# Retention and channel mix on one core: the order of instructions taken from a list schedule computed when the kernel is built

## The chip, the cores and the metric

The kernel runs on one core of a Trainium2 chip. A core has five engines with instruction streams of their own: PE (TensorE, matrix products into PSUM), DVE (VectorE), ACT (ScalarE), POOL (GpSimd) and SP (SyncE, which here only issues DMAs). Each engine takes its instructions in the order in which they were written into its stream, and waits at an instruction until what it needs has been signalled by the others. The metric is the device time of one execution, in microseconds (us); lower is better.

## What is computed

A retention layer (a linear attention with a decaying state) over q, k and v of shape 4 x 8 heads x 768 x 64, and then a channel mix (RWKV's feed-forward part) over its output, as 4 x 768 x 512:

```python
gamma = 1.0 - 2.0 ** (-5.0 - np.arange(H))
for t in range(S):
    state = gamma * state + einsum('bhd,bhe->bhde', k[:, :, t], v[:, :, t])
    y[:, :, t] = 1 / sqrt(D) * einsum('bhd,bhde->bhe', q[:, :, t], state)
x = y.transpose(0, 2, 1, 3).reshape(B, S, H * D)
x_prev = concatenate([0, x[:, :-1]], axis=1)
xk = mu_k * x + (1 - mu_k) * x_prev
xr = mu_r * x + (1 - mu_r) * x_prev
k = maximum(xk @ w_k, 0)            # 512 -> 1024
v = k * k @ w_v                     # 1024 -> 512
r = 1 / (1 + exp(-(xr @ w_r)))      # 512 -> 512
out = r * v
```

## The kernel before

A batch's 768 positions are cut into six chunks of 128 for the attention and into three blocks of 256 for the channel mix: 24 chunks and 12 blocks in all. Numbering below is over the whole run (chunk 0 to 23, block 0 to 11); block m needs chunks 2m and 2m + 1.

*A chunk* (`attention`, lines 105 to 167). Three DMAs bring q, k and v as 256 KB each into `t32` (line 100). DVE scales q and k by powers of gamma into float16, `qks` (line 108); POOL casts v (line 112). PE transposes `qks` in eight pieces into PSUM, `pT` (line 116), and ACT copies that out as `qkT` (line 118). PE forms the scores `pA` (line 123), DVE masks them in two halves into `a2t` (line 129). PE adds up the state `pS` from this chunk's k and v (line 136) and, through a product with the identity, the old state (line 142); DVE scales it into `s_new` (line 147). The output `pY` is the old state times q (line 155) plus scores times v (line 161); ACT copies it into `xT`, the transposed activations of the batch (line 166).

*A block* (`moe_block`, lines 169 to 223). POOL takes the difference of neighbouring positions, `dx` (line 174). DVE mixes it with mu into `x16` for k and for r, four instructions each (line 179). PE multiplies by w_k into four tiles `pZ`, 32 matmuls (line 192); ACT applies the ReLU into `krel` (line 196) and squares pairs of tiles into `k2` (line 201). For each half of the block's positions PE forms `pR` (four matmuls, line 206), ACT its sigmoid `rsb` (line 211), PE `pV` (eight matmuls, line 214), DVE the product of the two, `osb` (line 219), and SP issues the store (line 223).

*The order.* The program is written chunk after chunk, with a block behind every second chunk and the weights' loads and casts behind chunk 0. Tile's scheduler then sets each engine's order and the waits. PSUM is divided by pools: two banks shared by `pT`, `pS` and `pY`, two for `pA`, four for the block's tiles. On SP, the loads of chunk 1 stand behind the three weight loads (5.2 MB).

Of the kernel before, what the change touches and what calls it, by code (L numbers as in the profile page):

```python
# [9 lines left out]
F16 = mybir.dt.float16  # L10
# [4 lines left out]
KSC = 64.0  # L15


@with_exitstack
def kernel(
# [12 lines left out]
    nc = tc.nc  # L32
# [26 lines left out]
    wpool = ctx.enter_context(tc.tile_pool(name="weights", bufs=1))  # L59
    xpool = ctx.enter_context(tc.tile_pool(name="xstage", bufs=2))  # L60
# [3 lines left out]
    psX = ctx.enter_context(tc.tile_pool(name="psX", bufs=2, space=bass.MemoryType.PSUM))  # L64
    psA = ctx.enter_context(tc.tile_pool(name="psA", bufs=2, space=bass.MemoryType.PSUM))
    psM = ctx.enter_context(tc.tile_pool(name="psM", bufs=4, space=bass.MemoryType.PSUM))

# [4 lines left out]
    nc.sync.dma_start(out=c32, in_=c32d.ap())  # L72
    nc.sync.dma_start(out=c16, in_=c16d.ap())
# [5 lines left out]
    nc.sync.dma_start(out=mu[:, 0], in_=moe_mu_k.rearrange("(co ci) -> ci co", ci=P))  # L79
    nc.sync.dma_start(out=mu[:, 1], in_=moe_mu_r.rearrange("(co ci) -> ci co", ci=P))  # L80

    wk16 = wpool.tile([P, NCO, dff], F16, name="wk16")
    wv16 = wpool.tile([P, NFO, dm], F16, name="wv16")
    wr16 = wpool.tile([P, NCO, dm], F16, name="wr16")

    def load_weights():
        wk32 = wpool.tile([P, NCO, dff], F32, name="wk32")
        wr32 = wpool.tile([P, NCO, dm], F32, name="wr32")
        wv32 = wpool.tile([P, NFO, dm], F32, name="wv32")
        nc.sync.dma_start(out=wk32, in_=moe_w_k.rearrange("(co ci) f -> ci co f", ci=P))  # L90
        nc.sync.dma_start(out=wr32, in_=moe_w_r.rearrange("(co ci) e -> ci co e", ci=P))
        nc.sync.dma_start(out=wv32, in_=moe_w_v.rearrange("(fo fi) e -> fi fo e", fi=P))
        nc.vector.tensor_copy(out=wk16, in_=wk32)
        nc.scalar.copy(out=wr16, in_=wr32)
        nc.gpsimd.tensor_copy(out=wv16, in_=wv32)

    def load(b, c):
        t = ld.tile([P, 3, H, D], F32, tag="qkv32")
        for i, src in enumerate((q, k, v)):
            nc.sync.dma_start(  # L100
                out=t[:, i], in_=src[b, :, c * C : (c + 1) * C, :].rearrange("h t d -> t h d")
            )
        return t

    def attention(b, c, xT, s_prev):
        t32 = load(b, c)
        qks = awork.tile([P, 2, H, D], F16, tag="qks")
        nc.vector.tensor_tensor(  # L108
            out=qks, in0=t32[:, 0:2], in1=Gqk.unsqueeze(3).broadcast_to([P, 2, H, D]), op=ALU.mult
        )  # L110
        v16 = awork.tile([P, H, D], F16, tag="v16")
        nc.gpsimd.tensor_copy(out=v16, in_=t32[:, 2])  # L112
        pT = psX.tile([P, 2, NJ, C], F16, tag="px")
        for j in range(NJ):
            for i in range(2):
                nc.tensor.transpose(pT[:, i, j, :], qks[:, i, 2 * j : 2 * j + 2, :], ident)  # L116
        qkT = awork.tile([P, 2, NJ, C], F16, tag="qkT")
        nc.scalar.copy(out=qkT, in_=pT)  # L118
        pA = [psA.tile([P, NJ, C], F32, tag="pA", name=f"pA{hp}") for hp in range(2)]
        for j in range(NJ):  # L120
# [104 lines left out]
    for b in range(B):  # L225
# [3 lines left out]
        for c in range(NCH):  # L229
            s_prev = attention(b, c, xT, s_prev)  # L230
            if b == 0 and c == 0:
                load_weights()
# [32 lines left out]
```

## Time and profile before

| | |
|---|---|
| median of 2 runs | 259.45 us (259.04 to 259.86) |
| the profiled execution | 260.24 us |
| its span, first to last instruction | 257.6 us |
| busy: PE, DVE, ACT, POOL | 189.0, 126.7, 104.6, 42.3 us |
| mean granted clock of PE | 0.878 |
| moved by DMA | 30.73 MB, 119 GB/s over the span |

The span is what the profile shows; the rest of an execution's time lies around it. In the rows of the profile a group is named by its line, engine, operation and tiles (`pT<-c_sb,qks` is written from the constants and `qks`; buffer numbers and digits are left out, so `x16` reads `x`, `k2` reads `k`, `t32` reads `t`). Behind it stand the count, and in brackets the time for which the engine had waited just before, with what released it. PE is a matmul, PEld the load of its stationary operand, which overlaps. SPq is SP issuing a DMA. Rows of busy time by stretch give start and end, length, the engines' busy times with their instruction counts, the granted clock of PE (1.00 is full), the busy share of the DMA engines, and GB/s. Ends of matmuls are modelled.

### The profile page before, as it was taken

How to read it: one execution, taken by the hardware profiler on the slowest of the kernel's cores; microseconds unless marked ns; L12 is line 12 of the kernel's file. 1: busy time of each engine (PE TensorE's matmuls, PEld its weight loads, DVE VectorE, ACT ScalarE, POOL GpSimd, SP SyncE). 2: the span in 40 equal slices, each digit the busy share in tenths (PEclk: the TensorE clock that was granted, in tenths of full speed). 3: DMA queues.
4: the chain of work that ended last, by engine and by line, in shares of the span. 5: the costliest groups of instructions: out<-in, count | busy, mean ns of one | idle time of the engine just before them, and what ended most of it. 6: DMA issues, size and time to landing. Idle time of an engine off the chain costs nothing. (4 is left out here: it accounts for less than half of the span.)

```text
span 257.6 us, 3978 instructions
## 1 busy us (share of the span) xinstructions
PE 189.0 (73%) x1632; PEld 118.4 (46%) x1632; DVE 126.7 (49%) x217; ACT 104.6 (41%) x147; POOL 42.3 (16%) x41
## 2 busy tenths in 40 slices
PE   0300677779859969869679899789699599797394
PEld 0200445446336446455455564555464464563251
DVE  0431547357366375574680681771672762542422
ACT  1130221924534535337317326435345445344070
POOL 0105340030040040040130230310310400200200
PEclk9999999997986997999958959959869959779598
DMA  5999995149396374655366266265341101101002
GB/s 101 371 371 279 219 213 130 41 137 192 90 213 150 80 168 88 158 119 104 108 122 125 81 122 125 94 116 129 101 95 43 41 3 41 41 3 67 15 0 81
DMA packets 81793, 30.73 MB, mean 119 GB/s; under 512 B 76528, under 2 KB 76656, under 8 KB 81776
## 3 DMA queue, kind: packets, MB, share of 16 engines
q1 hardware_dynamic: 81776, 30.50, 49.7%
q8 instruction: 12, 0.20, 0.3%
q14 instruction: 5, 0.04, 0.0%
HBM read 24.20 MB, written 6.29 MB: 118 GB/s over the span
## 5 line engine op out<-in xcount | busy, mean ns | idle before, releaser
L192 PE MATMUL pZ<-x,wk 128*128 128x256 f16 x384 | 66.3, 354 | 13.8 <-DVE x L179 13.8
L192 PEld LDWEIGHTS <-wk 128*128 128x128 f16 x384 | 48.3, 126 | 30.8 <-issue 14.3
L219 DVE SCALAR_TENSOR_TENSOR osb<-pV,rsb 128x512 f32<-128x512 f32 x24 | 16.6, 691 | 75.4 <-ACT rsb L211 58.9
L214 PE MATMUL pV<-wv,k 128*128 128x512 f16 x192 | 45.5, 380 | 3.7 <-ACT k L201 3.7
L118 ACT COPY qkT<-pT 128x1024 f16<-128x1024 f16 x24 | 24.3, 1012 | 58.2 <-PE pT L116 58.2
L196 ACT ACTIVATE krel<-pZ 128x512 f32<-128x512 f32 x48 | 27.0, 591 | 51.0 <-PE pZ L192 51.0
L179 DVE SCALAR_TENSOR_TENSOR x<-dx,mu,xT 128x256 f16<-128x256 f32 x96 | 41.8, 504 | 10.7 <-POOL dx L174 10.7
L112 POOL CAST v<-t 128x512 f16<-128x512 f32 x24 | 16.3, 679 | 151.0 <-PE pY L161 74.1
L129 DVE TENSOR_TENSOR a2t<-pA,c_sb 128x512 f16<-128x512 f32 x48 | 30.9, 685 | 18.2 <-PE pA L123 18.0
L108 DVE TENSOR_TENSOR qks<-t,c_sb 128x1024 f16<-128x1024 f32 x24 | 30.1, 1256 | 16.0 <-DMA t<-in_k_dram 15.5
L116 PE MATMUL pT<-c_sb,qks 128*128 128x128 f16 x192 | 17.1, 235 | 23.4 <-DVE qks L108 23.2
L214 PEld LDWEIGHTS <-k 128*128 128x128 f16 x192 | 17.8, 98 | 29.0 <-ACT k L201 9.2
L174 POOL TENSOR_TENSOR dx<-xT 128x1024 f32<-128x1024 f32 x12 | 22.7, 1894 | 36.4 <-ACT xT L166 20.0
L166 ACT COPY xT<-pY 128x512 f32<-128x512 f32 x24 | 14.1, 589 | 33.4 <-PE pY L161 33.4
L116 PEld LDWEIGHTS <-qks 128*128 128x128 f16 x192 | 13.3, 105 | 27.4 <-DVE qks L108 23.9
L201 ACT ACTIVATE k<-krel 128x1024 f16<-128x1024 f32 x24 | 25.4, 1058 | 0.4
L206 PE MATMUL pR<-wr,x 128*128 128x512 f16 x96 | 24.6, 379 | 0.0
L161 PE MATMUL pY<-a2t,v 128*64 128x128 f16 x192 | 15.9, 249 | 9.7 <-DVE a2t L129 9.7
L123 PE MATMUL pA<-qkT 64*128 64x128 f16 x192 | 10.8, 240 | 14.2 <-ACT qkT L118 13.5
L161 PEld LDWEIGHTS <-v 128*64 128x64 f16 x192 | 10.2, 121 | 14.6 <-issue 10.8
L211 ACT ACTIVATE rsb<-pR 128x512 f32<-128x512 f32 x24 | 14.4, 601 | 1.4 <-PE pR L206 1.4
L123 PEld LDWEIGHTS <-qkT 64*128 64x128 f16 x192 | 6.0, 101 | 17.8 <-ACT qkT L118 17.8
(18 smaller groups left out, 63.8 us busy)
## 6 DMA issues: line engine op xcount, KB each, us to landing
t<-in_q_dram SPq DMA_DIRECT2D x24, 256.0 KB, 3.4
t<-in_k_dram SPq DMA_DIRECT2D x24, 256.0 KB, 4.2
t<-in_v_dram SPq DMA_DIRECT2D x24, 256.0 KB, 4.5
out_dram<-osb SPq DMA_DIRECT2D x24, 256.0 KB, 2.0
wk<-in_moe_w_k_dram SPq DMA_DIRECT2D x1, 2048.0 KB, 8.6
wv<-in_moe_w_v_dram SPq DMA_DIRECT2D x1, 2048.0 KB, 15.6
wr<-in_moe_w_r_dram SPq DMA_DIRECT2D x1, 1024.0 KB, 10.0
c_sb<-c SPq DMA_DIRECT2D x1, 64.0 KB, 2.0
```

Of the source, the lines that this page charges most:

```text
L108: nc.vector.tensor_tensor(out=qks, in0=t32[:, 0:2], in1=Gqk.unsqueeze(3).broadcast_to([P, 2, H, D]), op=ALU.mult)
L116: nc.tensor.transpose(pT[:, i, j, :], qks[:, i, 2 * j : 2 * j + 2, :], ident)
L118: nc.scalar.copy(out=qkT, in_=pT)
L129: nc.vector.tensor_tensor(out=a2t[:, hp], in0=pA[hp], in1=causal4, op=ALU.mult)
L161: nc.tensor.matmul(pY[hp * 64 : hp * 64 + 64, j, :], lhsT=v16[:, 2 * j + hp, :], rhs=a2t[:, hp, j, :], start=(j == 0 and c == 0), stop=(j ...
L174: nc.gpsimd.tensor_tensor(out=dx, in0=xcur, in1=xprev, op=ALU.subtract)
L179: nc.vector.scalar_tensor_tensor(out=x16[:, co], in0=dx[:, co], scalar=mu[:, w, co : co + 1], in1=xprev[:, co], op0=ALU.mult, op1=ALU.add,)
L192: nc.tensor.matmul(pZ[:, f], lhsT=wk16[:, co, fo * P : fo * P + P], rhs=xk16[:, co, :], start=(co == 0), stop=(co == NCO - 1),)
L196: nc.scalar.activation(out=krel[:, 2 * fp : 2 * fp + 2], in_=pZ, func=AF.Relu, scale=KSC)
L201: nc.scalar.activation(out=k2[:, hs], in_=krel[:, hs], func=AF.Square)
L206: nc.tensor.matmul(pR, lhsT=xr16[:, co, ts], rhs=wr16[:, co, :], start=(co == 0), stop=(co == NCO - 1),)
L214: nc.tensor.matmul(pV, lhsT=k2[:, fo, ts], rhs=wv16[:, fo, :], start=(fo == 0), stop=(fo == NFO - 1),)
```

## The change

Every step becomes a task of a small planner, `Plan`, with an engine, a duration and a latency in ns that are written into the program, a priority (`key`), the tasks it comes after, and the buffers it takes or uses. `order()` plays the tasks through: at each moment, an idle engine takes the task of lowest key that is ready and whose buffers are free. Then the tasks are written out by start time, inside `tc.manual_schedule()`, so that each engine's stream is the planner's. Nothing of the planner runs on the chip.

```diff
+class Plan:
+    LAT = {"PE": 260, "ACT": 110, "DVE": 110, "POOL": 160, "DMA": 2000}
...
+    def order(self):
...
+                    for t in left[e]:
+                        r = ready(t)
+                        if r is None:
+                            continue
+                        if r > now:
+                            heapq.heappush(events, r)
+                            continue
+                        t.start, t.end = now, now + t.dur
...
+        self.tasks.sort(key=lambda t: (t.start, t.idx))
...
+    LA = 3.0
+
+    def attention(b, c, xb, prev):
+        g = b * NCH + c
+        key = g - LA
...
+        e_T = add("PE", 460, key, do_T, after=[e_qks, k_c16], takes=[pT], uses=[qks])
...
+    def moe_block(b, m, xb, e_x):
+        g = b * NCH + (m + 1) * CPB - 1
...
+    span = plan.order()
+    with tc.manual_schedule():
+        plan.emit()
```

The key of a chunk's steps is its number less three, that of a block's the number of its last chunk: of steps that are ready, a chunk's come first until the attention is three chunks ahead. PE's tasks are whole groups: the transposes, `pS` with the identity products, `pA`, `pY`, each of the four `pZ`, each `pR`, each `pV`. The work is otherwise the same, with these differences:

```diff
-    ld = ctx.enter_context(tc.tile_pool(name="ld", bufs=3))
-    awork = ctx.enter_context(tc.tile_pool(name="awork", bufs=3))
-    mwork = ctx.enter_context(tc.tile_pool(name="mwork", bufs=2))
...
+    pool_of("t32", 4, [P, 3, H, D], F32)
+    pool_of("v16", 4, [P, H, D], F16)
...
+    pool_of("krel", 3, [P, 4, TM], F32)
+    pool_of("k2", 4, [P, 4, TM], F16)
+    pool_of("rsb", 3, [P, dm], F32)
+    pool_of("osb", 3, [P, dm], F32)
+    pool_of("px", 2, [P, 512], F32, PS)
+    pool_of("pA", 1, [P, 2, NJ, C], F32, PS)
+    pool_of("pm", 4, [P, 512], F32, PS)
```

`px` holds `pT`, `pS` and `pY` as before, and `pA` keeps its two banks; `pm` has the block's four. `krel` and `k2` are halves now, three and four of them in place of two whole ones. The loads and casts of w_k and w_v come in two halves each; of the casts of w_v one is on ACT and one on POOL, before it was one on POOL. The masked half of `pY` runs head parity by head parity. `mu` loads behind chunk 0, the weights behind chunk 1, and chunk 2 behind the weights.

The start of SP's stream before (`t_94` is chunk 0's tile, `t_156` chunk 1's, `t_315` chunk 2's; `mu` stands ahead):

```order
L100 DMA t_94<-in_q_dram 128x8x64
L100 DMA t_94<-in_k_dram 128x8x64
L100 DMA t_94<-in_v_dram 128x8x64
L90 DMA wk32_147<-in_moe_w_k_dram 128x4x1024
L91 DMA wr32_148<-in_moe_w_r_dram 128x4x512
L92 DMA wv32_149<-in_moe_w_v_dram 128x8x512
L100 DMA t_156<-in_q_dram 128x8x64
L100 DMA t_156<-in_k_dram 128x8x64
L100 DMA t_156<-in_v_dram 128x8x64
L100 DMA t_315<-in_q_dram 128x8x64
```

The weights stand between chunk 0 and chunk 1. Now, from behind the constants and chunk 0's q and k (`t32_126` is chunk 0's tile, `t32_132` chunk 1's, `t32_283` chunk 2's):

```order
L254 DMA t32_126<-in_v_dram 128x8x64
L219 DMA mu_60<-in_moe_mu_k_dram 128x4x1
L220 DMA mu_60<-in_moe_mu_r_dram 128x4x1
L254 DMA t32_132<-in_q_dram 128x8x64
L254 DMA t32_132<-in_k_dram 128x8x64
L254 DMA t32_132<-in_v_dram 128x8x64
L213 DMA wk32_64<-in_moe_w_k_dram 128x4x512 x2
L213 DMA wr32_66<-in_moe_w_r_dram 128x4x512
L213 DMA wv32_65<-in_moe_w_v_dram 128x4x512 x2
L254 DMA t32_283<-in_q_dram 128x8x64
```

Chunk 1's loads moved ahead of the weights, `mu` behind chunk 0. A little further on, where chunk 4's tile is loaded, stores stand among the loads:

```order
L254 DMA t32_324<-in_v_dram 128x8x64
L254 DMA t32_371<-in_q_dram 128x8x64
L438 DMA out_0_dram<-osb_373 128x512
L254 DMA t32_371<-in_k_dram 128x8x64
L254 DMA t32_371<-in_v_dram 128x8x64
L438 DMA out_0_dram<-osb_423 128x512
```

Block 0's first store is now ahead of chunk 4's k; before, the first two stores stood behind the q load of chunk 7.

ACT's stream in the steady part before, from one block's end through the next block:

```order
L211 ACTIVATE rsb_734<-pR_729 128x512
L118 COPY qkT_820<-pT_811 128x1024
L118 COPY qkT_979<-pT_970 128x1024
L166 COPY xT_748<-pY_850 128x4x128
L166 COPY xT_748<-pY_1009 128x4x128
L196 ACTIVATE krel_880<-pZ_882 128x512
L196 ACTIVATE krel_880<-pZ_892 128x512
L201 ACTIVATE k2_881<-krel_880 128x1024
L196 ACTIVATE krel_880<-pZ_903 128x512
L196 ACTIVATE krel_880<-pZ_913 128x512
L211 ACTIVATE rsb_929<-pR_924 128x512
```

Two chunks' copies come in a row, then the block's activations. Now, over a block in the middle of the run (`px` is `pT` for a `qkT` and `pY` for an `xT`, `pm` is `pZ` or `pR`):

```order
L408 ACTIVATE krel_1084<-pm_1060 128x512
L408 ACTIVATE krel_1084<-pm_1073 128x512
L344 COPY xT_123<-px_1088 128x4x128
L413 ACTIVATE k2_1133<-krel_1084 128x1024
L408 ACTIVATE krel_1147<-pm_1120 128x512
L408 ACTIVATE krel_1147<-pm_1137 128x512
L431 ACTIVATE rsb_1178<-pm_1149 128x512
L344 COPY xT_123<-px_1158 128x4x128
L413 ACTIVATE k2_1199<-krel_1147 128x1024
L277 COPY qkT_1223<-px_1180 128x1024
L431 ACTIVATE rsb_1241<-pm_1192 128x512
L277 COPY qkT_1243<-px_1204 128x1024
```

The copies of chunks moved in between the activations of a block. PE's stream goes with it. Before, a block's 56 matmuls follow each other, and then two chunks' steps. Now, over the same stretch, PE's groups read: two `pZ`, `pY`, `pA`, two `pZ`, `pR`, `pY`, transposes, `pR`, transposes, one `pZ` of the next block, `pV`, `pA`, `pV`, `pS`.

DVE's stream before, over one block:

```order
L108 TENSOR_TENSOR qks_1454<-t_1450,c32_sb_82 128x1024
L219 SCALAR_TENSOR_TENSOR osb_1164<-pV_1155,rsb_1153 128x512
L219 SCALAR_TENSOR_TENSOR osb_1183<-pV_1174,rsb_1172 128x512
L108 TENSOR_TENSOR qks_1613<-t_1609,c32_sb_82 128x1024
L129 TENSOR_TENSOR a2t_1280<-pA0_1270,c16_sb_83 128x512
L129 TENSOR_TENSOR a2t_1280<-pA1_1271,c16_sb_83 128x512
L129 TENSOR_TENSOR a2t_1426<-pA0_1416,c16_sb_83 128x512
L129 TENSOR_TENSOR a2t_1426<-pA1_1417,c16_sb_83 128x512
L179 SCALAR_TENSOR_TENSOR x16_1303<-dx_1301,mu_86,xT_748 128x256 x4
L179 SCALAR_TENSOR_TENSOR x16_1308<-dx_1301,mu_86,xT_748 128x256 x4
L147 TENSOR_TENSOR s_new_1438<-pS_1429,c32_sb_82 128x256
```

Both chunks' masks stand directly ahead of the mix that needs them. Now (`xk` and `xr` are the two mixes, `s16` is the state):

```order
L263 TENSOR_TENSOR qks_1315<-t32_1189,c32_sb_58 128x1024
L293 TENSOR_TENSOR a2t_1341<-pA_1319,c16_sb_59 128x512 x2
L263 TENSOR_TENSOR qks_1364<-t32_1254,c32_sb_58 128x1024
L381 SCALAR_TENSOR_TENSOR xk_1388<-dx_1343,mu_60,xT_123 128x256 x4
L381 SCALAR_TENSOR_TENSOR xr_1417<-dx_1343,mu_60,xT_123 128x256 x2
L318 TENSOR_TENSOR s16_1431<-px_1403,c32_sb_58 128x256
L381 SCALAR_TENSOR_TENSOR xr_1417<-dx_1343,mu_60,xT_123 128x256 x2
L263 TENSOR_TENSOR qks_1450<-t32_1362,c32_sb_58 128x1024
L434 SCALAR_TENSOR_TENSOR osb_1473<-pm_1433,rsb_1376 128x512
L293 TENSOR_TENSOR a2t_1476<-pA_1453,c16_sb_59 128x512 x2
L434 SCALAR_TENSOR_TENSOR osb_1502<-pm_1462,rsb_1446 128x512
```

The masks are one chunk's at a time, and the mix belongs to chunks whose `xT` was copied earlier; a `qks` stands between them.

More of the change, by code (lines that the diff above doesn't have):

```diff
@@ L1 @@
+import heapq
 from contextlib import ExitStack
@@ new lines, in attention @@
+        e_Y = add("PE", 500, key + 0.3, do_Y, after=e_m + [e_sprev], takes=[pY],
+                  uses=[v16, a2t, qkT] + ([s_prev] if c else []))
+        first = c == 0
+        if first:
+            z = add("DVE", 70, key, lambda: nc.vector.memset(xb.tile[:, :, 0:1], 0.0), takes=[xb])
+        e_x = add("ACT", 590, key + 0.3, lambda: nc.scalar.copy(
+            out=xb.tile[:, :, 1 + c * C : 1 + (c + 1) * C],
+            in_=pY.tile.rearrange("p (j t) -> p j t", j=NJ)),
+            after=[e_Y] + ([z] if first else []), uses=[xb, pY])
@@ L238 @@
+    span = plan.order()
+    print("plan", span)
+    with tc.manual_schedule():
+        plan.emit()
 _INS = ['q', 'k', 'v', 'moe_mu_k', 'moe_mu_r', 'moe_w_k', 'moe_w_v', 'moe_w_r']
```

421 lines of the change are left out of this document (277 added, 144 removed).

## The prediction

> **What bounds the kernel now.** I read the page's totals first, then busy time by stretch, then PE's instructions in order of time over one steady period, then the start and the end in the same view, and last the granted clock by stretch. The three stretches are: up to the first channel-mix matmul (41.86 us), from there to the first of the last block (243.32 us), and the rest.
>
> ```profile
> span 257.6 us, 3978 instructions
> PE 189.0 (73%) x1632; PEld 118.4 (46%) x1632; DVE 126.7 (49%) x217; ACT 104.6 (41%) x147; POOL 42.3 (16%) x41
> 0.00:41.86 41.86, 12.88 (x150) 9.12 (x150) 14.94 (x20) 8.99 (x9) 10.42 (x12) 1.00 1.04 255
> 41.86:243.32 201.46, 165.82 (x1427) 103.43 (x1427) 107.67 (x190) 90.55 (x130) 31.85 (x29) 0.85 0.42 97
> ```
>
> The columns after the length are PE, PEld, DVE, ACT, POOL, granted clock, DMA share, GB/s. For 42 us PE does 13 us of work while DMA is full. Then eleven block starts take 201.46 us, 18.3 each; DVE is busy 9.8 of those, ACT 8.2, POOL 2.9, and PE 15.1 at a mean clock of 0.85. So PE is the nearest bound, at a lowered clock and with holes. One period of PE shows the holes:
>
> ```profile
> 106.62 0.61 PE L116 MATMUL pT<-c_sb,qks 128*128 128x128 f16 x8
> 107.16 0.32 PE L136 MATMUL pS<-v,qks 128*64 128x64 f16 x8
> 107.41 0.29 PE L142 MATMUL pS<-s_new,c_sb 128*128 128x64 f16 x4
> 108.33 0.40 PE L123 MATMUL pA<-qkT 64*128 64x128 f16 x8 [0.64 <-ACT qkT L118]
> ...
> 110.84 0.40 PE L123 MATMUL pA<-qkT 64*128 64x128 f16 x8
> 111.17 0.32 PE L136 MATMUL pS<-v,qks 128*64 128x64 f16 x8
> 111.41 0.29 PE L142 MATMUL pS<-s_new,c_sb 128*128 128x64 f16 x4
> 111.63 0.41 PE L155 MATMUL pY<-qkT,s_new 64*64 64x128 f16 x8
> 112.01 0.22 PE L161 MATMUL pY<-a2t,v 128*64 128x128 f16 x1
> 112.61 0.38 PE L161 MATMUL pY<-a2t,v 128*64 128x128 f16 x7 [0.38 <-DVE a2t L129]
> 114.19 3.75 PE L192 MATMUL pZ<-x,wk 128*128 128x256 f16 x32 [1.20 <-DVE x L179]
> 117.78 1.03 PE L206 MATMUL pR<-wr,x 128*128 128x512 f16 x4
> 118.64 1.03 PE L214 MATMUL pV<-wv,k 128*128 128x512 f16 x4
> ...
> 131.09 6.39 PE L192 MATMUL pZ<-x,wk 128*128 128x256 f16 x32 [1.14 <-DVE x L179]
> ```
>
> Each matmul group's cost is the distance from its start to the next one's: transposes 0.54, pS 0.25, the identity product 0.22, pA 0.33, the state part of pY 0.38; the other part of pY never runs undisturbed, so 0.22 + 0.38 less two modelled tails of 0.07 (0.61 against 0.54 at the transposes) is 0.46. A chunk is 2.18 us. A block's pZ is 3.59 and each group of four 512-wide matmuls 0.86; with two of pR and four of pV, 8.75. A period, one block and two chunks, is 8.75 + 4.36 = 13.1 us of PE at full clock, and from Z to Z it is 131.09 - 114.19 = 16.9: 3.8 us of holes, all in the attention part, where PE waits on copies and masks. The second loss is the clock:
>
> ```profile
> 112.85:116.27 3.42, 2.22 (x25) 1.86 (x20) 2.93 (x7) 0.74 (x2) 1.01 (x2) 1.00 1.11 221
> 116.27:119.68 3.41, 3.41 (x25) 2.23 (x23) 2.11 (x4) 3.38 (x6) 0.00 (x0) 1.00 0.03 7
> 164.05:167.47 3.42, 2.33 (x44) 1.59 (x44) 1.79 (x3) 1.72 (x3) 2.36 (x2) 1.00 0.10 24
> 167.47:170.88 3.41, 2.41 (x12) 1.68 (x12) 3.26 (x8) 0.43 (x1) 0.67 (x2) 0.50 1.09 209
> ```
>
> The clock steps on a grid of 3.41 us. After the thin attention window at 164.05 (PE busy 2.33 of 3.42) it is halved, and the block that follows pays double: the pZ at 131.09 takes 6.39 for 3.75. Of the windows behind which it stayed full, the second pair shows one at 2.22, so no sharp threshold follows; full ones like 116.27 never lead to half.
>
> **The change, part by part.** *Start.* The second chunk's loads move ahead of the weights, and mu behind the first chunk.
>
> ```profile
> 1.60 0.50 SPq L79 DMA_DIRECT2D mu<-in_moe_mu_k_dram  x1
> 11.58 1.29 DVE L129 TENSOR_TENSOR a2t<-pA,c_sb 128x512 f16<-128x512 f32 x2 [0.92 <-PE pA L123]
> 13.36 2.29 DVE L93 CAST wk<-wk 128x4096 f16<-128x4096 f32 x1 [0.50 <-DMA wk<-in_moe_w_k_dram]
> 22.03 3.60 POOL L95 CAST wv<-wv 128x4096 f16<-128x4096 f32 x1 [12.82 <-DMA wv<-in_moe_w_v_dram]
> 24.52 2.19 DVE L108 TENSOR_TENSOR qks<-t,c_sb 128x1024 f16<-128x1024 f32 x1 [8.86 <-DMA t<-in_k_dram]
> 32.17 1.89 POOL L174 TENSOR_TENSOR dx<-xT 128x1024 f32<-128x1024 f32 x1 [2.28 <-ACT xT L166]
> 41.86 3.33 PE L192 MATMUL pZ<-x,wk 128*128 128x256 f16 x17 [0.85 <-DVE x L179]
> 240.86 1.89 POOL L174 TENSOR_TENSOR dx<-xT 128x1024 f32<-128x1024 f32 x1 [16.41 <-issue]
> 243.32 4.93 PE L192 MATMUL pZ<-x,wk 128*128 128x256 f16 x32 [3.22 <-DVE x L179]
> ```
>
> Before, chunk 1 is scaled (qks) only at 24.52, because its loads stood behind 5.2 MB of weights. Two mu loads of 0.5 us each leave the front, so chunk 0's masks end at 12.87 - 1.0 = 11.9, where chunk 1's qks now starts. From qks to dx took 7.65 us in chunk 1, about 1.0 of it a qks slowed beside the POOL cast; half of the wk cast (about 1.2) stands ahead of chunk 1's masks in the new order; from dx to pZ took 2.46 (240.86 to 243.32). First pZ: 11.9 + 6.7 + 1.2 + 2.5 = 22.3, before 41.86. PE runs at half clock there although the record says 1.00: 17 matmuls in 3.33 us are 196 ns each, against 112 in the 3.59 above. I add 1.7 us, half of one 3.4 us step, here and once more at the restart below.
>
> *Then a second hole.* Chunks 2 and 3 come behind the weights.
>
> ```profile
> 0.00:20.00 20.00, 2.85 (x32) 2.00 (x32) 5.33 (x7) 4.78 (x4) 1.02 (x5) 1.00 0.89 285
> 20.00:40.00 20.00, 9.02 (x104) 6.36 (x104) 7.88 (x9) 4.21 (x5) 8.79 (x6) 1.00 1.20 228
> t<-in_k_dram SPq DMA_DIRECT2D x24, 256.0 KB, 4.2
> L166 ACT COPY xT<-pY 128x512 f32<-128x512 f32 x24 | 14.1, 589 | 33.4 <-PE pY L161 33.4
> L108 DVE TENSOR_TENSOR qks<-t,c_sb x24: 1206/1215/2187, 7.5 to 209.0; 128x1024 f16<-128x1024 f32 x24
> ```
>
> Through chunk 2 there are 7.67 MB to move (0.79 a chunk, 5.24 of weights, 0.07 of constants): 5.70 by 20 us, the rest at 228 GB/s until 28.6, less the 1.0 of earlier start: 27.6. Chunk 3 comes 3.4 us later, at 31. Block 0: pZ from 22.3 takes 3.6 + 1.7, pR 1.7, chunk 2's transposes 0.5, the first pV 1.7, the output product 0.7: 32.2. Only then can SP issue the first out, which stands ahead of chunk 4's k load; that lands two issues (0.5 each) and 4.2 later, at 37.4. On DVE chunk 4's qks (1.2) stands ahead of chunk 3's masks (1.3): 39.9. pY 0.8, xT copy 0.6, dx to pZ 2.5, one more qks ahead of the mix 1.2: block 1's pZ at 45. By then block 0 and 5.3 chunks are done, where before nothing of block 0 and about 3.7 chunks were done at 41.86.
>
> *Steady part.* pZ, pR and pV groups now stand between an attention chunk's steps. What PE waited for is 0.64 on qkT, 0.38 twice on the masks, 1.20 on the mix: between transposes and pA there are now 3 us and more of other matmuls, and block and chunk are three chunks apart. I cost these waits at nothing; their cover is the channel mix, and it goes where none is left, in the last two blocks. What stays is unseen before: PE finding in-order DVE or ACT at another task. Where only pZ x8 and pR x4 (1.8 us) stand between pA and pY, the masks (1.29) just fit, and with a qks (1.2) or part of the mix ahead of them they do not. Ends: nothing, and the 3.8 us of today. I take 1.0 (two such waits of 0.5), nearer to the row with no wait, since DVE with 9.8 and ACT with 8.2 have 3 us to spare. Period 14.1.
>
> DVE's qks and mix now meet POOL's dx and v casts at any time; above, qks took 2.19 beside the cast of 22.03, where the median of its 24 is 1.2. If every POOL microsecond held DVE up, DVE would need 9.8 + 2.9 = 12.7 a period, still under 13.1; so nothing is added, and this is the second rival. The Trainium skill (SBUF — State Buffer, Who interferes with whom) says the same more strictly: a DVE instruction with two SBUF inputs and a GpSimd one that reads SBUF lock each other out for a whole instruction. The row agrees (blocked 1.1 us, until the cast ended at 25.63), and by it the sum would be between mine and that rival's.
>
> *End.* From the last pV to the end nothing changes:
>
> ```profile
> 251.12 2.78 PE pV L214 x12
> 253.99 0.69 DVE osb L219
> ```
>
> 257.6 - 253.9 = 3.7 us. The last two blocks run without attention, 17.5 us, plus 1.5 for the last chunk's copy, dx and mix behind 3.5 us of matmuls.
>
> *Sum.* 45 + 1.7 (cold) + 1.5 (0.7 chunk left over) + 9 x 14.1 + 19.0 + 3.7 = 197.8 of span. The profiled execution took 260.24 for its 257.6, so 2.6 more: **200 us**, against 260.24; the median of 259.45 lies 0.3% lower, which changes nothing.
>
> **Rivals.** *The half clock stays.* If PE's windows still thin out to 2.3 of 3.4 us, the mean is again 0.85: a period is 13.1/0.85 + 1.0 = 16.4, the last two blocks 20.6, in all 45 + 1.5 + 9 x 16.4 + 22.1 + 3.7 + 2.6 = 222. Against it: a 14.1 period is busy 93%, 3.2 of 3.41. For it: the windows up to 45 are thin, and where it once halves, everything is late. The Trainium skill (TensorE: Matmul & The Clock Gate, Part 1) halves the clock only after an idle window of some 3.4 us. By that rule this rival could not occur once PE runs; the row at 164.05 disagrees, halving after a window that was two thirds busy.
>
> *DVE becomes the bound.* POOL's 2.9 added to DVE's 9.8, the 1.0 of waits on DVE as well, and one qks a period that comes too late (1.2): 14.9, total 200 + 9 x 0.8 = 207. For it: the one overlap that the trace has was paid in full. Against it: 2.9 supposes that DVE always wants such operands while POOL works.
>
> *Slower: loads behind outs.* SP's order is fixed, and an out waits for its output product. If each period's loads were released only by the previous block's out, the period would be a chain: issue and landing 5.2, qks to dx 6.7, dx to pZ 2.5, pZ 3.6, pR and pV 5.2, output product 0.7: 23.9 us, and the total 45 + 1.5 + 9 x 23.9 + 19 + 3.7 + 2.6 = 287. It decides from a period of 21 us on. Against it: after the start the outs of a block stand among loads five or six chunks further on.
>
> *No change to speak of* would need periods of 20.7; the 3.8 us of holes and the half clock would both have to stay and something be added.
>
> **How the numbers follow.** Forecast case (188 to 212) 0.62; DVE bound 0.14; half clock 0.18; loads behind outs 0.03; stalls of both kinds up to no change 0.03. The likeliest gives 200. With no waits and the restart 3 us sooner it is 188; the range goes up to the half clock's 222, so 188 to 222 leaves out under 2 in 10. Faster by over 2% (about what a measurement of this kernel can tell from no change) 0.94, within 0.03, slower 0.03.
>
> **What would show it.** First pZ at 22, block 1's at 45 with a thin stretch between 33 and 45; pZ starts 14 us apart on average; granted clock near 1.00 from 50 us on; DVE busy about 70% of the steady stretch; mix and qks means up by under 15%. The prediction is wrong if pZ starts stay 16 us or more apart, or if PE's waits move to SP's loads.

## The result and the profile after

| | before | after |
|---|---|---|
| median of 2 runs | 259.45 us | 188.33 us (187.45 to 189.21) |
| ratio, 95% interval | | 0.726 (0.710 to 0.741) |
| profiled execution, its span | 260.24, 257.6 us | 189.21, 187.4 us |
| mean granted clock of PE | 0.878 | 0.971 |

The changed kernel takes 71.1 us less. The forecast was 200. In the later timing of experiments 11 and 12, one run of the changed kernel (191.52 us) and one of the kernel before (262.37) were in a slower state and are left out there. The page of the changed kernel gives the totals, and below them the granted clock in 40 equal slices of 4.7 us, in tenths:

```profile
span 187.4 us, 3984 instructions
PE 162.6 (87%) x1632; PEld 101.9 (54%) x1632; DVE 128.4 (69%) x218; ACT 105.5 (56%) x148; POOL 43.3 (23%) x41
PEclk9999999996579999999999999999999999999999
```

The other engines are busy about as long as before (DVE 1.7 us more). PE does the same matmuls in 26.4 us less, for the greater part because fewer of them run at half clock: summed over the stretches with a granted clock of 0.50, PE was busy for 51 us before and is for 8.4 now, and half of the difference is 21. There is one dip left, around 44 to 54 us, and none after it. The rest of the gain is PE's idle time, 24.8 us for 68.6. Busy time by stretch, with columns as before, from inside block 0 on, cut at the first pZ of block 1, of block 2 and of block 9:

```profile
33.00:46.45 13.45, 9.25 (x141) 6.27 (x141) 11.32 (x16) 4.20 (x6) 4.47 (x3) 0.89 0.85 202
46.45:65.83 19.38, 18.34 (x187) 11.13 (x185) 14.97 (x26) 10.50 (x15) 4.47 (x5) 0.81 0.64 149
65.83:153.18 87.35, 87.28 (x940) 55.19 (x937) 75.66 (x130) 56.74 (x84) 23.72 (x21) 1.00 0.68 166
153.18:172.25 19.07, 18.82 (x181) 12.28 (x180) 9.87 (x22) 13.62 (x21) 3.79 (x2) 1.00 0.11 42
```

From 65.83 to 153.18 us, seven periods of 12.5 us each, PE is idle for 0.07 us in all and at full clock. Before, a period was 18.3 us. PE's instructions in order of time at two places of these periods show how (`px` is `pT`, `pS` or `pY`; `pm` is `pZ` at L402, `pR` at L421, `pV` at L426):

```profile
92.40 0.40 PE L286 MATMUL pA<-qkT 64*128 64x128 f16 x8
92.73 1.92 PE L402 MATMUL pm<-xk,wk 128*128 128x256 f16 x16
94.48 1.03 PE L421 MATMUL pm<-wr,xr 128*128 128x512 f16 x4
95.44 0.42 PE L334 MATMUL px<-a2t,v 128*64 128x128 f16 x8
95.80 0.62 PE L274 MATMUL px<-c_sb,qks 128*128 128x128 f16 x8
...
106.03 0.40 PE L286 MATMUL pA<-qkT 64*128 64x128 f16 x8
106.36 1.05 PE L402 MATMUL pm<-xk,wk 128*128 128x256 f16 x8
107.25 1.03 PE L421 MATMUL pm<-wr,xr 128*128 128x512 f16 x4
108.21 0.41 PE L329 MATMUL px<-qkT,s 64*64 64x128 f16 x8
```

No row carries a wait. Between the scores `pA` at 92.40 and the masked part of `pY` at 95.44 stand 2.7 us of pZ and pR, and behind the scores at 106.03 still 1.9; before, only the chunk's own `pS` and the state part of its `pY` stood there (111.17 to 112.01), and PE waited 0.38 us for the masks. Nearly all the waits that are left lie ahead of 54 us. PE's waits summed by what it waited for, in the changed kernel (total, times, longest):

```profile
PE px L274 <- DVE qks L263: 10.0, 5, 7.1
PE pm L402 <- DVE xk L381: 3.5, 2, 3.2
PE px L334 <- DVE a2t L293: 3.1, 4, 1.6
PE pA L286 <- ACT qkT L277: 1.8, 3, 0.7
PE px L329 <- ACT qkT L277: 1.3, 2, 0.6
```

and in the kernel before:

```profile
PE pT L116 <- DVE qks L108: 23.2, 4, 13.3
PE pZ L192 <- DVE x L179: 13.8, 12, 3.2
PE pA L123 <- ACT qkT L118: 13.5, 19, 1.2
PE pY L161 <- DVE a2t L129: 9.7, 27, 0.8
```

Waits on the mix, the copies and the masks sank from 37.0 to 9.7 us. What stays is the start, where every load is still on its way.

### The profile page after: what moved, and what is told of

It is laid out like the page before. It is cut to its first block, busy times and chain, and to the rows that moved or that the text cites. A ratio compares the mean times of both kernels' runs of the same rounds, so it can differ in the third digit from the quotient of the medians.

```text
span 187.4 us, 3984 instructions
## 1 busy us (share of the span) xinstructions
PE 162.6 (87%) x1632; PEld 101.9 (54%) x1632; DVE 128.4 (69%) x218; ACT 105.5 (56%) x148; POOL 43.3 (23%) x41
## 5 line engine op out<-in xcount | busy, mean ns | idle before, releaser
L402 PE MATMUL pm<-xk,wk 128*128 128x256 f16 x384 | 52.9, 289 | 4.0 <-DVE xk L381 3.5
L426 PE MATMUL pm<-wv,k 128*128 128x512 f16 x192 | 45.4, 380 | 1.1 <-ACT k L413 1.1
L402 PEld LDWEIGHTS <-wk 128*128 128x128 f16 x384 | 37.6, 103 | 14.0 <-issue 6.3
L277 ACT COPY qkT<-px 128x1024 f16<-128x1024 f16 x24 | 24.3, 1011 | 30.9 <-PE px L274 30.9
L408 ACT ACTIVATE krel<-pm 128x512 f32<-128x512 f32 x48 | 28.3, 598 | 23.8 <-PE pm L402 23.1
L263 DVE TENSOR_TENSOR qks<-t,c_sb 128x1024 f16<-128x1024 f32 x24 | 30.9, 1295 | 8.0 <-DMA t<-in_k_dram 8.0
L381 DVE SCALAR_TENSOR_TENSOR xk<-dx,mu,xT 128x256 f16<-128x256 f32 x48 | 23.0, 537 | 11.4 <-POOL dx L374 11.4
L434 DVE SCALAR_TENSOR_TENSOR osb<-pm,rsb 128x512 f32<-128x512 f32 x24 | 16.5, 688 | 18.2 <-PE pm L426 12.8
L426 PEld LDWEIGHTS <-k 128*128 128x128 f16 x192 | 17.6, 98 | 20.6 <-ACT k L413 2.0
L274 PE MATMUL px<-c_sb,qks 128*128 128x128 f16 x192 | 16.4, 235 | 10.0 <-DVE qks L263 10.0
L421 PE MATMUL pm<-wr,xr 128*128 128x512 f16 x96 | 24.2, 379 | 0.0
L381 DVE SCALAR_TENSOR_TENSOR xr<-dx,mu,xT 128x256 f16<-128x256 f32 x48 | 22.2, 516 | 0.0
L274 PEld LDWEIGHTS <-qks 128*128 128x128 f16 x192 | 13.1, 105 | 14.2 <-DVE qks L263 10.8
L431 ACT ACTIVATE rsb<-pm 128x512 f32<-128x512 f32 x24 | 14.4, 602 | 2.0 <-PE pm L421 2.0
L421 PEld LDWEIGHTS <-xr 128*128 128x128 f16 x96 | 8.9, 98 | 6.7
```

Of the source, the lines that this page charges most:

```text
L263: e_qks = add("DVE", 1250, key, lambda: nc.vector.tensor_tensor(out=qks.tile, in0=t32.tile[:, 0:2], in1=Gqk.unsqueeze(3).broadcast_to([P, ...
L274: nc.tensor.transpose(o[:, i, j, :], qks.tile[:, i, 2 * j : 2 * j + 2, :], ident)
L277: e_qkT = add("ACT", 1010, key, lambda: nc.scalar.copy(out=qkT.tile.rearrange("p a j c -> p (a j c)"), in_=pT.tile.bitcast(F16)), after=[e ...
L381: nc.vector.scalar_tensor_tensor(out=o.tile[:, co], in0=dx.tile[:, co], scalar=mu[:, w, co : co + 1], in1=prv()[:, co], op0=ALU.mult, op1= ...
L402: nc.tensor.matmul(o[:, f], lhsT=wk16[:, co, fo * P : fo * P + P], rhs=xk.tile[:, co, :], start=(co == 0), stop=(co == NCO - 1))
L408: e_r.append(add("ACT", 595, g + 0.2 + 0.1 * fp, lambda f2=f2, pZ=pZ, krel=krel: nc.scalar.activation(out=krel.tile[:, 2 * f2 : 2 * f2 + 2 ...
```

## Experiments

The theory behind the prediction (A in the expectations): PE's groups of block and chunk stand alternately, so that the one covers the copies and masks of the other, which takes away the holes and with them the half clock. The rivals (B, where an expectation uses the letter) put the gain down to something else that came with the change: the load order at the start, more buffers and halves, the lookahead by itself, or the exact times written into the planner. Each kernel below ran once beside the kernel before (258.35, 260.31 and 260.71 us there) unless more is said. The changed kernel's own runs, here and in experiment 12, lie between 187.45 and 190.44 us, so a single run within that band shows no difference.

**1. The start alone.** The kernel before, with chunk 1's loads ahead of the weights and mu behind chunk 0; nothing else.

```diff
-    nc.sync.dma_start(out=mu[:, 0], ...)
-    nc.sync.dma_start(out=mu[:, 1], ...)
...
+    early = [load(0, 0)]
+    nc.sync.dma_start(out=mu[:, 0], ...)
+    nc.sync.dma_start(out=mu[:, 1], ...)
+    early.append(load(0, 1))
...
-        t32 = load(b, c)
+        t32 = early[c] if b == 0 and c < 2 else load(b, c)
```

> The kernel before with one edit: chunk 1's loads stand ahead of the weights on SP, mu behind chunk 0. My account gives the start some 20 of the 71 us: the first pZ moves from 41.9 to about 23 us, but the second hole opens (chunks 2 and 3 land at 27 and 31 us), so that block 1's pZ comes at about 45 to 48 instead of 59, with periods of 17 to 18.5 us behind it as before. Expected 244 to 250 us. If the start carried most of the gain, this kernel would come to 215 or less; if the start only moved work around that the holes lose again, it stays at 257 or more.

It took 243.13 us, 15.2 less than before. Its pZ groups, two at the start and one in the steady part:

```profile
21.83 5.24 PE L195 MATMUL pZ<-x,wk 128*128 128x256 f16 x32 [4.25 <-DVE x L182]
43.26 6.35 PE L195 MATMUL pZ<-x,wk 128*128 128x256 f16 x32 [1.48 <-DVE x L182]
114.83 6.40 PE L195 MATMUL pZ<-x,wk 128*128 128x256 f16 x32 [1.14 <-DVE x L182]
```

The first pZ comes at 21.83 as in the changed kernel, block 1's at 43.26, even sooner than there; the periods behind it stay as they were, with waits and half clock (0.877 over the span). The start is worth 15 us to the old order, and the other 56 come from elsewhere.

**2. Everything but the order.** The changed kernel with its buffers, halves and load order, but the steps written chunk after chunk and left to Tile.

```diff
-    span = plan.order()
-    with tc.manual_schedule():
-        plan.emit()
+    loads = [t for t in plan.tasks if t.eng == "DMA" and t.key < -1.35]
+    loads.sort(key=lambda t: t.key)
+    plan.tasks = loads + [t for t in plan.tasks if t not in loads]
+    plan.emit()
```

> The changed kernel's tiles, buffers, halves of weights and order of loads, but without the computed order: its steps are written chunk after chunk and block after block, and Tile sets each engine's order. If the order is what fills the holes, the periods go back to 17 to 18.5 us at a mean clock of about 0.85, and with the better start the time is 240 to 250 us. If the buffers (four t32, halves of krel and k2, three rsb and osb) carried the steady gain, it is 190 to 200 us.

242.26 us. That is 0.9 under experiment 1, which has none of the buffers and halves, so those are worth next to nothing in this order; what they are worth to the planned order was not run. Blocks follow each other every 17.5 us, as expected. The mean clock is 0.929, higher than the 0.85 expected, so that what is lost here lies mostly in holes. PE's waits are back:

```profile
PE pm L402 <- DVE xk L381: 18.6, 14, 3.2
PE pA L286 <- ACT qkT L277: 11.8, 19, 1.1
PE px L334 <- DVE a2t L293: 8.4, 26, 1.1
```

The order of the instructions, with the same instructions and buffers, is worth 242.26 - 188.33 = 54 us.

**3. No lookahead.** `LA = 0`, with the keys of mu and the weights raised by 3, so that the loads stay in order.

```diff
-    LA = 3.0
+    LA = 0.0
```

> The changed kernel with LA = 0 (the priorities of loads of mu and weights moved by three with it, so that the start of SP's stream stays as it is): the key no longer puts a chunk three ahead of a block. Theory A: a planner that takes any ready task when the engine is idle runs ahead by itself as far as buffers allow, so that PE still has other matmuls for each wait; 187 to 198 us, periods 12.6 to 13.5. Theory B: the lookahead of three is what hides the chain from the scores to the mix (7 us and more); then waits of 2 us and more a period come back and it is 205 to 225 us.

198.75 us, between the two theories: 10 us slower than the changed kernel, 43.5 faster than the written order. PE's largest wait but the start's:

```profile
PE pm L402 <- DVE xk L381: 5.9, 5, 3.2
```

and a place where it costs more than its length:

```profile
105.92 6.01 PE L402 MATMUL pm<-xk,wk 128*128 128x256 f16 x32 [0.67 <-DVE xk L381]
```

Here and there chunk steps still stand in a row ahead of a block, PE runs out of work, and the block behind is at half clock for most of its pZ (6.01 us for 3.75). Three chunks of lookahead are worth some 10 us; without them most of the gain still stands, although a block's four pZ now often stand together (all 32 matmuls at 105.92) and mostly only pR and pV take turns with the chunks.

**4. The clock by itself.** The kernel before, with useless 128-wide matmuls: 12 ahead of each chunk's scores, 22 ahead of each block's first pZ. They write banks that the real matmuls overwrite.

```diff
+        for i in range(12):
+            nc.tensor.matmul(pA[0][:, 0], lhsT=ident, rhs=ident, start=True, stop=True)
...
+            for i in range(22 if fp == 0 else 0):
+                nc.tensor.matmul(pZ[:, 0, 0:P], lhsT=ident, rhs=ident, start=True, stop=True)
```

> The kernel before with matmuls of no use in its holes: 12 of 128 columns for each chunk and 22 for each block, on the constants, into PSUM that the next real product overwrites. The work that counts is the same. If the half clock comes from thin windows on PE, the granted clock stays near 1.00 in the steady part, a period falls from 18.3 to 17 to 17.5 us and the time to 242 to 250 us. If the half clock comes on its own after a time of load, or if only windows that are idle throughout would bring it, the mean clock stays about 0.85 and the time is 259 or more.

250.55 us, 7.8 less than before with 552 matmuls more, and 0.5 over what was expected. Its granted clock by slice (6.2 us each):

```profile
PEclk9855578999999999999999999999999999999979
```

With its thin windows filled, PE is at full clock from about 45 us to the last block. A period is still 17.5 us, for 18.3 before. The one period of the kernel before that had the full clock nearly throughout, from 114.19 to 131.09, took 16.9, so the filler probably costs some time of its own. Measured, the clock alone is worth 8 us; without the filler's cost it would be at most 11 x (18.3 - 16.9) = 15, an estimate. Either is well under 54: the holes had to be filled with work that is needed.

**5. Lookahead without mixing.** The planner as it is, with one rule more: once PE has begun a block it takes nothing else until the block's 56 matmuls are issued.

```diff
+            if t.eng == "PE" and run["left"] and t.blk != run["blk"]:
+                return None
...
+                e_Z.blk = g
...
+            e_R.blk = g
...
+            e_V.blk = g
```

> The changed kernel, planned with one more rule: once PE has begun a block, it does nothing else until the block's last pV (lookahead of three chunks kept, other engines planned to suit). It separates running ahead from mixing the groups. If what fills the holes is that pZ, pR and pV stand between an attention chunk's steps, holes of 1.5 to 3 us a period come back between the blocks, some windows thin out and halve the clock, and the time is 205 to 228 us. If the lookahead alone does it (each step's inputs are old by the time PE comes to it), it stays at 188 to 195 us.

221.57 us, 33 slower than the changed kernel. Busy time over 105 us of its steady part, and a row of PE in it:

```profile
65.00:170.00 105.00, 90.31 (x872) 56.56 (x872) 75.12 (x123) 53.62 (x77) 23.72 (x21) 0.91 0.53 131
117.39 0.40 PE L299 MATMUL pA<-qkT 64*128 64x128 f16 x8 [1.45 <-DVE a2t L306]
```

PE is idle for 14.7 of 105 us. The planner's lookahead is the same, but the attention's steps stand next to each other again and wait for the copies and masks (3.4 and 3.5 us in this stretch), and the next block for its mix (5.4). So the planned order with whole blocks takes 21 us off the written order (242.26), and letting the groups alternate takes the other 33.

**6. An early first block undone.** The changed kernel with all weights ahead of chunk 1, as before the change, planned anew.

```diff
-        d = add("DMA", 2900, -2.0 + 0.1 * i, dma(wk32...
+        d = add("DMA", 2900, -3.0 + 0.1 * i, dma(wk32...
-    d = add("DMA", 2900, -1.6, dma(wr32, wrd))
+    d = add("DMA", 2900, -2.8, dma(wr32, wrd))
-        d = add("DMA", 2900, -1.5 + 0.1 * i, dma(wv32...
+        d = add("DMA", 2900, -2.7 + 0.1 * i, dma(wv32...
```

> The changed kernel with the loads of the weights back ahead of chunk 1, as before the change; everything is planned anew for it. The prediction gave the earlier first pZ 20 us of gain. Theory A: the start is bound by the bytes to be moved in any case (8.5 MB until chunk 3 is in), and PE has all of it done at about the same time in either order; first pZ at 33 to 36 us, but steady from 46 to 50, and the time 188 to 194 us. Theory B: the early first pZ is worth what it is early by; 198 to 202 us.

189.91 us. Its busy time from the first pZ on:

```profile
37.75:45.50 7.75, 7.75 (x83) 5.50 (x81) 6.28 (x10) 5.18 (x9) 3.17 (x3) 1.00 1.03 235
45.50:180.00 134.50, 134.17 (x1390) 84.28 (x1387) 105.76 (x185) 87.55 (x129) 32.53 (x28) 1.00 0.54 137
```

The first pZ is at 37.75 instead of 21.71, 16 us later, and the time is within the changed kernel's own runs (its span is 187.9 us, for 187.4). From that pZ on PE never waits for long, and its clock is full by 45.5, where the changed kernel is still in its half-clock stretch. What the early block 0 gains is spent in the hole behind it. So chunk 1's place ahead of the weights, worth 15 us to the old order, is worth nothing that these runs can tell to the planned one: once PE is the bound, the date of the first pZ hardly counts, and the date from which PE is dense does.

**7. Chunks 2 and 3 ahead of w_r and w_v.** The changed kernel, planned with 1200 ns for a chunk's load and 2650 for a weight's (1400 and 2900 before).

```diff
-    d = add("DMA", 2900, -1.6, dma(wr32, wrd))
+    d = add("DMA", 2650, -1.05, dma(wr32, wrd))
-        d = add("DMA", 2900, -1.5 + 0.1 * i, dma(wv32...
+        d = add("DMA", 2650, 0.0 + 0.02 * i, dma(wv32...
```

> The changed kernel with chunk 2's loads ahead of w_r, chunk 3's ahead of w_v, and DMA durations in the planner of 1200 and 2650 ns for 1400 and 2900. If the second hole (33 to 46 us) comes from chunks 2 and 3 landing behind the weights and from chunk 4's k standing behind the first out, block 1's pZ comes at 36 to 41 us and the time is 179 to 185 us. If the hole comes from PE's slow clock and the in-order chains there, block 1's pZ stays at 44 or later and the time at 186 to 190.

185.4 us. Block 1's pZ came at 44.79, not at the 36 to 41 expected, and the time lies between the two forecasts. DVE, POOL and PE ahead of it:

```profile
37.14 2.97 DVE L263 TENSOR_TENSOR qks<-t,c_sb 128x1024 f16<-128x1024 f32 x1 [3.29 <-DMA t<-in_k_dram]
...
37.13 1.89 POOL L374 TENSOR_TENSOR dx<-xT 128x1024 f32<-128x1024 f32 x1
...
40.16 1.04 PE L274 MATMUL px<-c_sb,qks 128*128 128x128 f16 x8 [1.53 <-DVE qks L263]
40.99 3.07 PE L426 MATMUL pm<-wv,k 128*128 128x512 f16 x8
```

DVE waited 3.29 us for the load of chunk 4, whose qks stands ahead of the mix, and then the qks stood still until POOL's dx had ended (37.13 + 1.89 = 39.02, and 1.1 of its own make 40.1). PE's transposes waited 1.53 us for it. Behind them block 0's last pV ran mostly at half clock (3.07 us, where eight such matmuls took 1.9 in the changed kernel), and only then came block 1's pZ. From 44.79 on PE is dense at full clock; that and 1.7 us of earlier start are the gain.

**8. Only the clock of the start.** The changed kernel, with useless matmuls (into `pA`'s banks) that the planner puts where PE is idle from 12 to 20 and 28 to 44 us of its plan.

```diff
+    for a, b in [(12000.0, 20000.0), (28000.0, 44000.0)]:
+        for i in range(60):
+            warms.append(buf("pA"))
+            add("PE", 8 * 56, 60.0, lambda i=len(warms) - 1: warm(i), after=[k_c16],
+                takes=[warms[-1]], lat=0).win = (a, b)
```

> The changed kernel with matmuls of no use (on the constants, into pA's banks, overwritten later) in PE's planned idle time from 12 to 20 us and from 28 to 44 us. If thin windows halve the clock, it is full from about 17 us on and does not halve at 44; the first pZ x32 takes 3.6 to 4 us for 6.3, block 1's groups run at full speed, and the time falls by 4 to 8 us, to 180 to 185. If the filler only stands in the way of the real work or the clock halves all the same, 188 to 194.

190.52 us; 180 to 185 was expected if the clock was what held the start, 188 to 194 if the filler stood in the way. Block 0's pZ ran warm, and yet:

```profile
23.55 3.66 PE L410 MATMUL pm<-xk,wk 128*128 128x256 f16 x32
42.61 1.28 PE L461 MATMUL pA<-c_sb 128*128 128x128 f16 x16 [0.36 <-DVE a2t L301]
```

Filler stood ahead of real steps (L461): 1.2 us of it ahead of chunk 3's pY at 42.61, and 1.9 more at 38.84 ahead of its scores. Block 1's first pZ came 2.6 us later, at 49.1, and ran mostly at half clock even so. Block 0's warm pZ ended only 0.8 us sooner than in the changed kernel, and the filler delayed what came behind it, so this run does not settle what the half clock at the start costs by itself.

**9. Do the written-in durations matter?** Every step of PE, DVE, ACT and POOL planned as 1000 ns.

```diff
+            t.dur = 1000 if t.eng != "DMA" else t.dur
```

> The changed kernel, planned with 1000 ns for every step of PE, DVE, ACT and POOL in place of its own duration (DMA durations and all latencies kept). Theory A: with three chunks of lookahead PE's queue holds other groups for any wait, so that wrong durations cost little: 188 to 196 us, PE's waits in the steady part under 6 us in all. Theory B: the fit of masks and copies between PE's groups needs the right durations; waits of 1 us and more a period, 200 to 212 us.

189.2 us: 0.5% above the changed kernel's median and equal to its profiled execution. The steps really last from 0.33 us (`pA`) to 1.89 (`dx`), so the plan needs the dependencies, the buffers and the keys, but hardly the durations. This run took one rival, the exact times, away.

**10. The start tuned further.** Experiment 7 with the first constant's load planned as 1700 ns (100 before), 2900 ns for a weight's load, and k's mix ahead of the qks in priority.

```diff
-    k_c32 = add("DMA", 100, -9.0, ...
+    k_c32 = add("DMA", 1700, -9.0, ...
-                e_mix[w].append(add("DVE", 800, g + 0.1 + 0.5 * w, mix, ...
+                e_mix[w].append(add("DVE", 800, g - 4 + 4.6 * w, mix, ...
```

> As the run with chunk 2's loads ahead of w_r and chunk 3's ahead of w_v (185.4 us), with the planner's first landing 1.6 us later, 1200 ns for a load of 256 KB and 2900 ns for 1 MB, and the k mix ahead of any qks in priority. There chunk 4's qks stood ahead of block 1's mix on DVE, waited for its load and then ran beside dx (2.97 us for 1.22). If what is left of the hole is that order, block 1's pZ moves from 44.8 to 40 to 43 us and the time to 181 to 184; if it is the bytes (9.2 MB through chunk 4) alone, it stays at 185 to 187.

Block 1's pZ came at 42.16, as expected, 2.6 us sooner than in experiment 7, with the clock full all the way; but the time, expected at 181 to 184, was 185.48, the same. Busy time from there:

```profile
45.00:180.00 135.00, 132.04 (x1368) 82.90 (x1366) 104.52 (x183) 85.31 (x126) 32.83 (x28) 1.00 0.59 147
```

and in experiment 7:

```profile
44.79:180.00 135.21, 133.60 (x1388) 84.56 (x1384) 104.17 (x182) 86.84 (x127) 32.99 (x28) 1.00 0.58 144
```

PE is idle for 3.0 us there, where it was idle for 1.6: with the mix ahead, the chunks' qks come late, and PE waits for them (0.46 and 0.56 us right behind the block's start). The span became 1.1 us shorter (182.5 for 183.6), and what lies around it 1.2 longer, which one run can't tell from chance.

**11 and 12. The better start against the changed kernel.** Experiment 7's kernel and the changed kernel, unaltered, timed in three rounds beside the kernel before (259.62 us).

> The kernel with chunk 2's loads ahead of w_r and chunk 3's ahead of w_v again, timed over several rounds: 185 to 186 us, ratio to the kernel before 0.71 to 0.72, if the 3 us below the changed kernel are real; 188 to 189 if its one time was a low draw.

> The changed kernel itself beside it on the same chip: 187 to 189.5 us, ratio 0.72 to 0.73.

Experiment 7's kernel took 185.44 us (185.16 to 185.71), 0.715 of before with an interval of 0.709 to 0.720; the changed kernel 189.33 (188.58 to 190.44), or 0.731 with 0.724 to 0.737. The intervals do not meet: the load order of experiment 7 takes another 2.2% off (0.715 / 0.731), and it is the best version that was run.

## Why the prediction was right, and where it was off

The mechanism was right: PE's work became the bound of the steady part, and holes and half clock went together. The sizes were less so. The time of 188.33 lies 0.3 us above the low end of the range, and one of its two runs (187.45) below it, so that it is inside is luck. That end of 188 had been reckoned with no waits and a restart 3 us sooner; the waits did stay away, but the restart came 1.45 us later, and PE's work, put too high, made up for it. The terms of the sum against the changed kernel's span:

| step | predicted, us | measured, us |
|---|---|---|
| first pZ | 22.3 | 21.71 |
| block 1's first pZ | 45 | 46.45 |
| PE's work from there to the last pV | 136.9 | about 132.4 |
| waits in it | 10.5 | 1.4 |
| half clock in it | 1.7 | about 3.5 |
| end | 3.7 | 3.6 |
| span | 197.8 | 187.4 |

The predicted work is 9 x 13.1, 17.5 for the last two blocks and 1.5 for the chunk left over; the waits are 9 x 1.0 and the 1.5 of the last block; together with the 1.7 that is 149.1 us. Measured are 137.3 (from 46.45 to 183.75, where the last pV ends): the idle 1.4 us from the stretches above, half of the 7.0 us for which PE was busy at half clock from 46.45 to 53.84, and the rest.

*The start and the second hole* came nearly when they were worked out, the second 1.45 us later, but not by every step named. The first store did stand ahead of chunk 4's k load on SP, at 33.95 for the 32.2 worked out. That load was to hold chunk 4's qks, and with it chunk 3's masks. By the rows it was not waited for:

```profile
33.24 0.69 DVE L434 SCALAR_TENSOR_TENSOR osb<-pm,rsb 128x512 f32<-128x512 f32 x1 [4.40 <-PE pm L426]
35.37 1.22 DVE L263 TENSOR_TENSOR qks<-t,c_sb 128x1024 f16<-128x1024 f32 x1
38.11 1.22 DVE L263 TENSOR_TENSOR qks<-t,c_sb 128x1024 f16<-128x1024 f32 x1
...
31.77 0.61 POOL L267 CAST v<-t 128x512 f16<-128x512 f32 x1 [2.47 <-DMA t<-in_v_dram]
```

Chunk 3 had landed by 31.77, where POOL casts its v, but its qks ran only at 35.37: DVE stood at block 0's osb, which waited 4.40 us for pV, and did chunk 2's masks behind it. Chunk 4's qks followed at 38.11 without a wait for its load. Store and osb hang on the same pV, which is why the date came out near all the same. Chunk 3's masks then ended at 40.5 (39.9 worked out), the copy of its xT at 42.5 (41.3), and the qks of chunk 5 stood directly ahead of block 1's mix:

```profile
43.45 2.12 DVE L263 TENSOR_TENSOR qks<-t,c_sb 128x1024 f16<-128x1024 f32 x1
45.49 2.37 DVE L381 SCALAR_TENSOR_TENSOR xk<-dx,mu,xT 128x256 f16<-128x256 f32 x4
...
42.59 1.89 POOL L374 TENSOR_TENSOR dx<-xT 128x1024 f32<-128x1024 f32 x1 [2.79 <-ACT xT L344]
```

This qks was held up by 0.9 us beside POOL's dx (2.12 for 1.22). The working had charged a whole qks of 1.2 there, so from dx to pZ it came to 3.9 us for the 3.7 worked out. Experiment 6 adds that the early first pZ itself was worth nothing that could be measured, and experiment 7 that chunk 4's loads ahead of the first store bring block 1 only 1.7 us forward.

*The waits of a period* are the step that was mis-sized: 1.0 us was taken, between bounds of 0 and 3.8, and it is 0.07 us in seven periods, the lower bound. The place that the working feared exists, with one pZ and one pR between a chunk's `pA` (106.03, above) and `pY` (108.21), but the masks were in time there too: DVE began them at 106.48, with no other task ahead of them.

*PE's work in a period* was put at 13.1 us and is 12.5. Two things were counted too high, as the groups of the changed kernel show:

```profile
L329 PE MATMUL px<-qkT,s 64*64 64x128 f16 x160 | 8.4, 226 | 1.3 <-ACT qkT L277 1.3
L312 PE MATMUL px<-s,c_sb 128*128 128x64 f16 x64 | 4.8, 198 | 0.0
```

Twenty-four chunks would give 192 and 96, and `pS` has 160 for 192 as well: the first chunk of each batch has no old state and the last needs no new one, which was in the profile before as well. By the prediction's own durations that is 0.38 + 0.25 + 2 x 0.22 = 1.07 us a batch, 0.36 a period. And the masked part of pY, undisturbed, takes 0.36 us (95.44 to 95.80 above), for the 0.46 that was worked out: 0.20 a period. Together 0.56.

*The end of the run without cover* was charged 1.5 us for the last chunk's copy, dx and mix. It was not paid: block 10 began at 160.78, while block 9 and the last chunks were still in work, and PE was idle for 0.25 us of the 19.07 from 153.18 on.

*The cold clock* was charged 1.7 us at each of two starts. At the first it was 2.5 (pZ took 6.11 us from its start to the next group's, for 3.59), at the second about 3.5. So one half step was too little: at the second the clock stayed half behind a step of 3.41 us of which PE was busy for 3.0 (from 47.02) and came back behind one that was full (from 50.43). What it takes is not settled, since in the kernel before it came back behind a step with 2.65 us busy (from 242.56). In the working's reading of the clock two rows are mixed up: the stretch with 2.22 us busy and no halving behind it is in the first pair, at 112.85, and the thin stretch ahead of the pZ at 131.09 is the one from 126.50 to 129.92, with 1.81 us busy. The conclusion drawn there holds.

*DVE's share* was to be about 70% of the steady stretch and is 75.66 of 87.35, or 87%. The period is shorter than forecast, and DVE has 128.4 / 12 = 10.7 us a block, not the 9.8 that were read from a stretch ahead of which 3.7 chunks had already been done. DVE would be the next bound.

*The rivals.* The half clock did not stay: one stretch of 10 us besides the cold start. By experiments 4 and 5 it went because the holes went; where they stand again (experiment 5) the clock is back at 0.91. DVE did not become the bound through POOL: that rival priced POOL's overlap at 2.9 us a period, and DVE's whole busy time grew by 1.7 us (126.7 to 128.4), 0.14 a block. The mean of k's mix in the changed kernel, and of the mix in the kernel before:

```profile
L381 DVE SCALAR_TENSOR_TENSOR xk<-dx,mu,xT 128x256 f16<-128x256 f32 x48 | 23.0, 537 | 11.4 <-POOL dx L374 11.4
L179 DVE SCALAR_TENSOR_TENSOR x<-dx,mu,xT 128x256 f16<-128x256 f32 x96 | 41.8, 504 | 10.7 <-POOL dx L174 10.7
```

It is up by 7%, that of qks by 3% (1295 ns for 1256), under the 15% that were named. A load stood behind an out at the start, but DVE waits for loads only twice in all (8.0 us, for chunks 0 and 2), and PE never.

*What stays open.* Why the chain at the start cannot be shortened further was not settled: experiment 10 brought block 1 forward by 2.6 us and gave it back in small waits and around the span. What the half clock at the start costs by itself is open too (experiment 8), and whether the planned order would do with the buffers of before.

## What to carry to other kernels

Where PE's work comes in two streams, each of which waits on other engines between its steps, let their groups alternate in PE's order; here the lookahead and the exact durations mattered less than that, and a rough list schedule with right dependencies was enough. Cost such a plan at PE's work alone in the steady part, and put the care into the date from which PE is dense: a first product that is early but followed by a hole is worth little. Count a group's instructions over the whole run before its cost is multiplied by the periods.

## What the runs showed of the hardware

*The clock halves behind thin windows, not only behind idle ones.* In the changed kernel the stretches ahead of the half clock, on the grid of 3.41 us:

```profile
36.79:40.20 3.41, 2.16 (x45) 1.58 (x44) 2.83 (x5) 1.47 (x3) 1.03 (x1) 1.00 0.98 242
40.20:43.61 3.41, 2.12 (x45) 1.58 (x42) 2.10 (x5) 1.44 (x2) 1.02 (x1) 1.00 1.14 257
43.61:47.02 3.41, 1.95 (x14) 1.40 (x14) 3.41 (x4) 0.85 (x2) 2.52 (x3) 0.50 0.89 201
```

PE was busy for 2.12 us of the 3.41 before the clock was halved; a stretch with 2.16 had passed without. In the kernel before, one with 2.33 was followed by a halving, so no threshold of busy time can be read from these rows. The table of states in the Trainium skill (TensorE: Matmul & The Clock Gate, Part 1) names an idle window as the condition; no window here was idle, so the measurement goes against it as it did in the kernel before. The same part also tells of a kernel whose clock went up and down because PE was idle for short times between its groups, and that is nearer to what these rows show.

*DVE and POOL can hold each other up for a whole instruction.* In experiment 7 a qks that started 0.01 us after POOL's dx took 2.97 us, which is the dx (1.89) and its own 1.1; in the changed kernel one that started 0.86 us into a dx took 2.12. In experiment 10 it went the other way: a dx that started 0.01 us after a qks (1.23) took 2.97 for 1.89. The Trainium skill (SBUF — State Buffer, Who interferes with whom) describes this lock, and these rows agree. On the mean it costs little (1295 ns a qks for 1256 before); at the start of experiment 7 PE waited 1.53 us for such a qks.
